# Loading one of three inputs four tokens to a partition, and a weight in smaller pieces

## The chip, the cores and the metric

The kernel runs on one core of a Trainium2 chip. The metric is the device time of one execution in microseconds (us), lower is better. The median of three runs of the kernel before is 166.17 us.

## What is computed

Two layers follow each other, an RWKV-style linear attention and an MLP-Mixer block. Batch is 4, heads 8, sequence 768, head size 48 (so the model width is 384), hidden sizes 256 (over tokens) and 1536 (over channels).

```python
for t in range(S):                       # attention, per batch and head
    kt, vt, rt = k[:, :, t], v[:, :, t], r[:, :, t]
    cur = einsum('bhd,bhe->bhde', u * kt, vt)
    y[:, :, t] = einsum('bhd,bhde->bhe', rt, state + cur)
    state = w[..., None] * state + einsum('bhd,bhe->bhde', kt, vt)
x = y.transpose(0, 2, 1, 3).reshape(B, S, H * D)
u2 = x + (relu(x.T @ w_tok1) @ w_tok2).T # mixing over tokens
out = u2 + relu(u2 @ w_ch1) @ w_ch2      # mixing over channels
```

All inputs and the output are float32. k, r and v lie in memory as [batch, head, token, 48], so one token of one head is a run of 192 bytes.

## The kernel before

The attention is cut into 24 *units*, six per batch, of 128 tokens and all 8 heads each. A unit loads k, r and v, each with one DMA (direct memory access transfer) from the SyncE queue, into a tile of 128 partitions by 384 numbers: one token per partition, its eight heads side by side. Each such load is 1024 runs of 192 bytes, 192 KB in all. The decay w is put into two tables, `wn` for k and `wp` for r, with one column block per chunk position; both are made on ScalarE at the start, as exponentials of ln w (`lnw`) times a token number (`iota`). The products k·wn and r·wp go, in bfloat16, into a tile called `kpr` (steps `kp` and `rp`, on GpSimd or VectorE). For units 0 to 13 TensorE transposes the two halves of `kpr` into `tr_ps` (steps `trk`, `trr`), and ScalarE copies the result to `rk`, for some units in two halves (`rkk`, `rkr`) and for the others in one. For units 14 to 23 a transposing DMA does it. From `rk` come the masked scores (`at_ps`, `AT`), the output `y_ps` and the state `kv_ps`, `S`; `x_b` is the unit's result. v becomes `vb` in bfloat16 on ScalarE.

When a batch's six units are through, its token mixing follows (`h_ps` with `wtok`, `h1r`, then `uT` and `u_sb`), and then the channel mixing in two halves of three chunks: 12 steps `z` per half (`z_ps`, 128 of the 1536 hidden columns each, weights `wch1`), `zr` (relu), and `h` steps with `wch2` (`h_ps`), whose sum is stored (`osb`, `out_dram`).

The order is not written by hand. `graph` lists the steps with estimated durations, waits and ranks, `Plan.run` simulates them, and the steps are emitted in that order; each engine then works strictly through its own list. The SyncE list of loads is fixed by `CFG["transfers"]`. The weights are cast from float32 to bfloat16 by DMAs that GpSimd issues, each placed behind a step named in `CFG["wafter"]`: `wtok1` and `wtok2` behind the loads of unit 4, then the pieces of `wch1` and `wch2` behind `rp5`. They use a queue of their own (q0 in the profile, the SyncE loads are q1), and all queues share the core's 16 DMA engines. The load of k of unit 6 is held back until `y5` is through (`hold`), and a load of unit n+8 waits until unit n's buffer is free.

Where all engine calls go through one helper, all instructions carry one line number in the profile (L512); they are told apart by the names of their tiles.

Of the kernel before, what the change touches and what calls it, by code (L numbers as in the profile page):

```python
# [13 lines left out]
f32 = mybir.dt.float32  # L14
bf16 = mybir.dt.bfloat16
i32 = mybir.dt.int32
# [15 lines left out]
LATER = tuple(range(2 * C, NU))  # L32

# [127 lines left out]
MM = 0.1625  # L161
# [6 lines left out]
def graph(do, cfg):  # L168

    p = Plan(4, cfg.get("busy_until", dict(ACT=3.9, DVE=3.6, POOL=5.0, PE=5.4)), cfg.get("in_flight", 8), cfg.get("relax_from", 0.0))  # L170
# [10 lines left out]
    lnw = p.add("lnw", [("ACT", 0.49, 0.6)], rank=-100, emit=do("lnw"))  # L181
# [13 lines left out]
    for n, (kind, i) in enumerate(cfg["transfers"]):  # L195
# [11 lines left out]
    wx, wi = {}, {}  # L207

    def weight(i, after):
        wi[i] = s = p.add(f"i:w{i}", [("POOL", 0.9, cfg.get("wseen", 1.0), True)], after, rank=-50, emit=do("weight", i))  # L210
        took = cfg.get("wtime", (3.0, 2.6, 3.1, 7.7, 3.1) if 5 not in cfg["wafter"] else (3.0, 2.6, 3.1, 3.9, 3.1, 3.9))[i]
        wx[i] = p.transfer(f"x:w{i}", s, took, took + 1.0, -1.0)

    for i in cfg["wafter"]:
# [3 lines left out]
    for u in range(NU):  # L218
        b, c = divmod(u, C)
        r = unit_rank(u)  # L220
        f = cold[u] if u < len(cold) else 1.0
        tab = tables[c % G]
        t_at, t_y, t_yS = cfg.get("pe_times", ((0.36, 0.25, 0.185),) * 2)[u >= C]
        old = xs.get(u - LEAD)
        d = cfg.get("dve_late", {}).get("kr", 0.5) if u >= cfg.get("early", 6) else cfg.get("kr0", 0.5)
        DK = DVE2 + (d,)
        d = cfg.get("dve_late", {}).get("yd", 0.5) if u >= cfg.get("early", 6) else cfg.get("yd0", 0.5)
# [10 lines left out]
        if u in turned:  # L238
            s = p.add(f"i:t{u}", [("SP", 1.35, 1.4)], [kp, rp], rank=-2000, emit=do("turn_unit", u))
            rk = p.transfer(f"x:t{u}", s, 1.56, 2.2, 0.0)  # L240
        else:
# [80 lines left out]
    for b in range(B):  # L322
        r, m, o = mix_rank(b) + cfg.get("mix", (0.0,) * B)[b], mlp_rank(b), out_rank(b)
        f = 1.0
        h = None
# [16 lines left out]
        uT, some = [], []  # L342
# [27 lines left out]
        for sg in range(2):  # L370
            zr = []
            for j in range(NJ):
                old = downs[2 * b + sg - 3] if 2 * b + sg >= 3 else []
                z = p.add(f"z{b}_{sg}_{j}", [("PE", 3 * MM, 3 * MM + 0.13)], old + uT[3 * sg:3 * sg + 3] + [wx[2] if j < NJ // 2 else wx[4]], take=True, rank=m + 0.1 * sg + 0.001 * j, emit=do("z", b, sg, j))
# [57 lines left out]
    + [('u', 13)]  # L432
    + [('b', 0)]
    + [("u", u) for u in range(14, 24)]
    + [('w', 0), ('w', 1), ('w', 2), ('w', 4), ('w', 3), ('w', 5)],
# [6 lines left out]
    parts=2,  # L442
    cold=(1.8, 1.8, 1.8, 1.3),
    xload={6: 0.33},
    wtime=(3.0, 2.6, 3.1, 5.2, 3.1, 3.9),
    raw=(0, 1, 5, 8, 11),
    rk_two=(0, 1, 2, 3, 4, 6),
    mix=(0.0, 0.0, -1.0, -2.6),
# [17 lines left out]
def kernel(  # L466
# [13 lines left out]
    nc = tc.nc  # L480
# [5 lines left out]
    dch = moe_w_ch1.shape[1]  # L486
    by_pe = CFG.get("by_pe", range(NU))
    direct = CFG.get("direct", ())

    const = ctx.enter_context(tc.tile_pool(name="const", bufs=1))  # L490
    wts = ctx.enter_context(tc.tile_pool(name="wts", bufs=1))
# [29 lines left out]
    def h3(t):  # L521
        return t.rearrange("p (h d) -> p h d", h=H)
# [2 lines left out]
    idle = const.tile([128, 512], bf16, name="idle")  # L525
    dve.memset(idle, 0.0)
    row = const.tile([1, dm], f32, name="row")
    rows = const.tile([2 * HP, 2, P], f32, name="rows")
# [10 lines left out]
    w_ps = psM.tile([128, dm], f32, name="w_ps", tag="m")  # L539
# [6 lines left out]
    pe.matmul(w_ps, ones, row, start=True, stop=True)  # L546
    warm(CFG.get("warm", (1, 10))[1])

    iota_i = const.tile([128, 2, G], i32, name="iota_i")
# [4 lines left out]
    ident = const.tile([128, 128], bf16, name="ident")  # L554
    make_identity(nc, ident)
    mask = const.tile([128, 128], f32, name="mask")
    pool.memset(mask, 1.0)
    pool.affine_select(
# [34 lines left out]
    lnw = const.tile([128, dm], f32, name="lnw")  # L593
    wn = const.tile([128, G, dm], f32, name="wn")
    wp = const.tile([128, G, dm], f32, name="wp")
    wu_sb = const.tile([128, 2, HP], f32, name="wu_sb")
# [9 lines left out]
    def wp_(eng, g):  # L606
        act.activation(wp[:, g, :], lnw, Exp, scale=iota[:, 0, g:g + 1])

    def wu(eng):
# [24 lines left out]
    def load(eng, nm, i):  # L634
        b, c = divmod(i, C)
        t = lpool.tile([128, dm], f32, name=f"ld_{nm}")
        ins = sp.dma_start(h3(t), SRC[nm][b, :, ts(c, T), :].rearrange("h s d -> s h d"))
        if i in CFG.get("hold", {}) and nm == "k":
            first = INS["".join(map(str, CFG["hold"][i]))]
            tc.add_manual_dep(ins.ins, first.ins.name,  # L640
                              mybir.DependencyInfo(mybir.DependencyClass.Sync, mybir.DependencyReason.DATA),
                              reason="weights first")
        loaded[nm, i] = t

    def weight(eng, i):
        t, src = [(wtok1, moe_w_tok1), (wtok2, moe_w_tok2), (wch1, moe_w_ch1), (wch2, moe_w_ch2), (wch1, moe_w_ch1), (wch2, moe_w_ch2)][i]
        cols = {2: slice(0, dch // 2), 4: slice(dch // 2, dch)}.get(i, slice(None))
# [11 lines left out]
        ENG[eng].tensor_mul(kprs[i % NB][:, 0, :, 0:D], h3(loaded["k", i]), h3(wn[:, i % G, :]))  # L659

    def rp(eng, i):
        ENG[eng].tensor_mul(kprs[i % NB][:, 1, :, 0:D], h3(loaded["r", i]), h3(wp[:, i % G, :]))

    def vb(eng, i):
        L[i]["vb"] = apool.tile([128, dm], bf16, name="vb")
        INS[f"vb{i}"] = act.copy(L[i]["vb"], loaded["v", i])

# [27 lines left out]

    def rk(eng, i):
        L[i]["rk"] = apool.tile([128, 2, HP, T], bf16, name="rk")
        (act.copy if eng == "ACT" else dve.tensor_copy)(L[i]["rk"], L[i]["tr"])

    def rkp(eng, i, j):  # L700
        if "rk" not in L[i]:
            L[i]["rk"] = apool.tile([128, 2, HP, T], bf16, name="rk")
        (act.copy if eng == "ACT" else dve.tensor_copy)(L[i]["rk"][:, j], L[i]["tr"][:, j])

    def atq(eng, i, q):
        if q == 0:
# [234 lines left out]
    def do(kind, *args):  # L941
        return lambda eng: STEPS[kind](eng, *args)
# [53 lines left out]
```

## Time and profile before

| | |
|---|---|
| median of 3 runs (lowest, highest) | 166.17 us (164.99, 168.54) |
| the profiled execution's span | 166.5 us |
| TensorE busy | 156.8 us, 94% of the span |
| VectorE, ScalarE, GpSimd busy | 106.8, 87.2, 65.3 us |
| DMA: bytes moved, packets | 26.26 MB, 97427 |

The profile lists for the profiled execution no time beside its span. Busy time is the sum of an engine's instructions; the chain of waits follows the last instruction back to what released it, step by step. "SPq" and "POOLq" are DMA instructions as their engines issue them, "DMA" is the transfer itself, and a DMA share of 1.0 means that 16 DMA engines had packets under way on average. A wait in square brackets stands behind the instruction that ended it, with what released it.

### The profile page before, as it was taken

To read this page: it belongs to the slowest core of one execution; us is meant where nothing else is said; L and a number is where in the kernel's file an instruction comes from. 1 tells how busy PE (TensorE), PEld (TensorE's weight loads), DVE (VectorE), ACT (ScalarE), POOL (GpSimd) and SP (SyncE) were. 2 spreads that over 40 slices of the span, in tenths; PEclk is the share of its full clock that TensorE was granted. 3 is DMA by queue.
4 is the path that set the end of the run, shared out by engine and by line. 5 is a ranking of instruction groups with operands and counts; after the bars stand their busy time and mean duration, and the time that the engine had idled before them with its cause. 6 is when DMAs were issued, how large, how long until landed. Compare 5 with 4: busy or idle time off the path is not lost.

```text
span 166.5 us, 3791 instructions
## 1 busy us (share of the span) xinstructions
PE 156.8 (94%) x1462; PEld 100.6 (60%) x1464; DVE 106.8 (64%) x219; ACT 87.2 (52%) x182; POOL 65.3 (39%) x80
## 2 busy tenths in 40 slices
PE   6797999599999999999999999999999999999991
PEld 1377764356677666666666665666656655665671
DVE  5189996300459989899989889977885582021031
ACT  3996743279198636579804452069154502904900
POOL 7839970000009647386785857103840000000000
PEclk9999999789999999999999999999999999999999
DMA  5999999999699899999999994999990028012012
GB/s 100 215 213 210 159 187 176 188 184 168 131 208 287 158 192 216 217 230 182 198 192 169 230 158 106 188 235 222 171 240 6 4 50 218 16 51 94 0 47 94
DMA packets 97427, 26.26 MB, mean 158 GB/s; under 512 B 90753, under 2 KB 97410, under 8 KB 97410
## 3 DMA queue, kind: packets, MB, share of 16 engines
q1 hardware_dynamic: 93920, 22.88, 67.2%
q0 software_dynamic: 3488, 3.15, 12.3%
q8 instruction: 11, 0.18, 0.5%
q14 instruction: 6, 0.05, 0.1%
q10 hardware_dynamic: 2, 0.00, 0.0%
HBM read 20.65 MB, written 4.72 MB: 152 GB/s over the span
## 4 chain that ended last, share of the span: by engine, by line
PE 79%; DMA 8%; POOL 5%; ACT 3%; issue 2%; DVE 1%; SPq 1%; POOLq 0%
PE h_ps L512 31%; PE z_ps L512 29%; DMA wch<-in_moe_w_ch_dram 6%; PE y_ps L512 4%; PE at_ps L512 4%; PE hT_ps L512 3%; PE tr_ps L512 3%; POOL kpr L512 3%; PE kv_ps L512 2%; DMA ld_v<-in_v_dram 2%; PE t_ps L512 1%; ACT rk L512 1%; POOL wtok L512 1%; SPq L512 1%; POOL yd L512 0%
## 5 line engine op out<-in xcount | busy, mean ns | idle before, releaser
L512 ACT ACTIVATE zr<-z_ps 128x384 bf16<-128x384 f32 x94 | 45.5, 492 | 47.5 <-PE z_ps L512 47.3
L512 PE MATMUL z_ps<-uT,wch 128*128 128x384 bf16 x288 | 53.6, 331 | 2.0 <-DMA wch<-in_moe_w_ch_dram 2.0
L512 PE MATMUL h_ps<-wch,zr 128*128 128x384 bf16 (+1 forms) x300 | 52.5, 319 | 0.0
L512 PEld LDWEIGHTS <-wch 128*128 128x128 bf16 x288 | 27.0, 99 | 18.8 <-DMA wch<-in_moe_w_ch_dram 2.4
L512 PEld LDWEIGHTS <-zr 128*128 128x128 bf16 x300 | 27.9, 98 | 15.5 <-issue 0.2
L512 POOL TENSOR_TENSOR yd<-vb,adg 128x384 f32<-128x384 bf16 x18 | 15.5, 860 | 46.5 <-ACT adg L512 27.9
L512 DVE TENSOR_TENSOR AT<-at_ps,mask 128x512 bf16<-128x512 f32 x43 | 27.9, 682 | 0.7 <-PE at_ps L512 0.6
L512 DVE TENSOR_TENSOR osb<-u_sb,h_ps 128x384 f32<-128x384 bf16 (+1 forms) x22 | 11.7, 533 | 23.4 <-PE h_ps L512 23.3
L512 POOL TENSOR_TENSOR kpr<-ld_r,wp 128x384 bf16<-128x384 f32 x16 | 16.6, 1036 | 5.3 <-ACT wp L512 2.8
L512 ACT COPY rk<-tr_ps 128x512 bf16<-128x512 bf16 (+1 forms) x20 | 15.0, 756 | 4.9 <-PE tr_ps L512 4.5
L512 PEld LDWEIGHTS <-kpr 128*128 128x128 bf16 x192 | 13.7, 107 | 6.0 <-POOL kpr L512 2.6
L512 DVE TENSOR_TENSOR x_b<-y_ps,yd 128x384 bf16<-128x384 f32 x24 | 13.2, 552 | 5.2 <-PE y_ps L512 5.1
L512 POOL TENSOR_TENSOR kpr<-ld_k,wn 128x384 bf16<-128x384 f32 x15 | 15.2, 1011 | 1.8 <-DMA ld_r<-in_r_dram 0.7
L512 PEld LDWEIGHTS <-rk 48*128 48x128 bf16 (+1 forms) x272 | 11.0, 99 | 6.4 <-issue 2.7
L512 ACT CAST vb<-ld_v 128x384 bf16<-128x384 f32 x24 | 12.3, 511 | 4.3 <-POOL kpr L512 3.1
L512 PE MATMUL tr_ps<-ident,kpr 128*128 128x128 bf16 x112 | 12.1, 245 | 2.4 <-ACT rk L512 1.4
L512 DVE TENSOR_TENSOR S<-kv_ps,bm 128x384 bf16<-128x384 f32 x13 | 7.2, 551 | 6.0 <-PE kv_ps L512 5.8
L512 DVE TENSOR_TENSOR u_sb<-x_b,hT_ps 128x384 bf16<-128x384 bf16 x21 | 10.4, 546 | 0.9 <-PE hT_ps L512 0.9
L512 PEld LDWEIGHTS <-wtok 128*128 128x128 bf16 x90 | 8.0, 98 | 4.8 <-issue 0.6
L512 PEld LDWEIGHTS <-AT 128*128 128x128 bf16 x192 | 8.4, 98 | 3.4 <-DVE AT L512 0.8
L512 PE MATMUL at_ps<-rk 48*128 48x128 bf16 x192 | 10.2, 229 | 0.2 <-ACT rk L512 0.2
L512 PE MATMUL h_ps<-x_b,wtok 128*128 128x384 bf16 x48 | 10.2, 326 | 0.0
(81 smaller groups left out, 145.4 us busy)
## 6 DMA issues: line engine op xcount, KB each, us to landing
ld_k<-in_k_dram SPq DMA_DIRECT2D x24, 192.0 KB, 3.8
ld_r<-in_r_dram SPq DMA_DIRECT2D x24, 192.0 KB, 3.8
ld_v<-in_v_dram SPq DMA_DIRECT2D x24, 192.0 KB, 3.8
out_dram<-osb SPq DMA_DIRECT2D x23, 192.0 KB, 2.6
wch<-in_moe_w_ch_dram POOLq DMA_DIRECT2D x4, 576.0 KB, 14.2
wtok<-in_moe_w_tok_dram POOLq DMA_DIRECT2D x2, 384.0 KB, 6.4
u_bc<-in_u_dram SPq DMA_DIRECT2D x1, 192.0 KB, 5.0
out_dram<-osb SPq DMA_DIRECT2D x2, 96.0 KB, 1.6
```

Source lines behind the costliest of these rows:

```text
L512: ins = tc.keep_in_program_order(f(*args, **kw))
```

## The change

For units 0 to 13 (`split`), r is loaded by two DMAs instead of one. Each takes four of the eight heads (every second one) and puts four consecutive tokens of one head behind each other in a partition: 128 partitions are 4 heads by 32 groups of tokens, and a run in memory is 4 x 48 numbers, 768 bytes. The source pattern of each is 4 heads, 32 groups, 192 numbers. In consequence

- the table `wp` gets the same layout (`wr`): a second small load of w (`row4`), a matmul with a matrix `quarter` that spreads four rows over the partitions, a second logarithm `lnr`, token numbers `iota_r`, three products on VectorE and an exponential in place. For units 14 to 23 the table is written again in the old layout (`wp_as_read`), from step `vb` of units 13 to 15.
- the product `rp` writes through a view of four dimensions, and the copy of r's half of `rk` puts the tokens back in order. `rk` of units 0 to 13 is always copied in two halves.

The first half of `wch1` (768 columns) is asked for as two pieces of 384 columns (weights 2 and 6); the first three `z` steps wait for the first alone.

```diff
+R = HP                                   # 4
...
-                z = ... [wx[2] if j < NJ // 2 else wx[4]] ...
+                z = ... [wx[2] if j < NJ // 4 else wx[6] if j < NJ // 2 else wx[4]] ...
...
-    wafter={0: 'x:r4', 1: 'x:r4', 2: 'rp5', 4: 'kp5', 3: 'rp5', 5: 'rp5'},
+    wafter={0: 'x:r4', 1: 'x:r4', 2: 'rp5', 6: 'rp5', 4: 'kp5', 3: 'rp5', 5: 'rp5'},
...
+    split=range(0, 14),
...
     act.dma_start(out=row, in_=w.rearrange("h d -> (h d)")[None, :])
+    act.dma_start(out=row4, in_=w.rearrange("(a q) d -> a (q d)", q=2))
...
+    pe.matmul(w_ps[:, dm:], quarter..., row4, start=False, stop=True, ...)
...
     def lnw_(eng):
-        act.activation(lnw, w_ps, Ln)
+        act.activation(lnr..., w_ps[:, dm:], Ln)
+        act.activation(lnw, w_ps[:, 0:dm], Ln)
+        for g in range(G):
+            dve.tensor_mul(wr[:, g], lnr..., iota_r[:, g]...)
...
     def wp_(eng, g):
+        act.activation(wp[:, g, :], wp[:, g, :], Exp)
...
-        ins = sp.dma_start(h3(t), SRC[nm][b, :, ts(c, T), :].rearrange("h s d -> s h d"))
+        src = SRC[nm][b, :, ts(c, T), :]
+        if nm == "r" and i in split:
+            for q in range(2):
+                ins = sp.dma_start(t[:, ts(q, dm // 2)], src.rearrange("(a q) (s j) d -> q a s (j d)", q=2, j=R)[q])
+        else:
+            ins = sp.dma_start(h3(t), src.rearrange("h s d -> s h d"))
...
     def rkp(eng, i, j):
...
+        if j == 1 and i in split:
+            to, src = to.rearrange("p a (t j) -> p a t j", j=R), src.rearrange("p j (a t) -> p a t j", a=HP)
```

The head of SyncE's list, with the loads of the first two units (a row's last number is the shape that the first operand takes), before:

```order
L512 DMA ld_k<-in_k_dram 128x8x48
L512 DMA ld_r<-in_r_dram 128x8x48
L512 DMA ld_v<-in_v_dram 128x8x48
L512 DMA ld_k<-in_k_dram 128x8x48
L512 DMA ld_r<-in_r_dram 128x8x48
```

and the same place now:

```order
L515 DMA ld_k<-in_k_dram 128x8x48
L515 DMA ld_r<-in_r_dram 128x1x192 x2
L515 DMA ld_v<-in_v_dram 128x8x48
L515 DMA ld_k<-in_k_dram 128x8x48
L515 DMA ld_r<-in_r_dram 128x1x192 x2
```

Each load of r has become two, in the same place; nothing else moves on this queue, through all 14 units.

On GpSimd, the stretch from the products of unit 4 to the weights (kpr_126 belongs to unit 4, kpr_118 to unit 5), before:

```order
L512 TENSOR_TENSOR kpr_126<-ld_k,wn 128x8x48
L512 DMA wtok_146<-in_moe_w_tok_dram 128x6x256
L512 TENSOR_TENSOR kpr_126<-ld_r,wp 128x8x48
L512 DMA wtok_147<-in_moe_w_tok_dram 128x2x768
L512 TENSOR_TENSOR kpr_118<-ld_k,wn 128x8x48
L512 TENSOR_TENSOR kpr_118<-ld_r,wp 128x8x48
L512 DMA wch_148<-in_moe_w_ch_dram 128x3x768 x2
L512 DMA wch_149<-in_moe_w_ch_dram 128x6x384 x2
```

and now (kpr_138 and kpr_130 are the same two buffers):

```order
L515 TENSOR_TENSOR kpr_138<-ld_k,wn 128x8x48
L515 DMA wtok_159<-in_moe_w_tok_dram 128x6x256
L515 TENSOR_TENSOR kpr_138<-ld_r,wp 128x2x4x48
L515 DMA wtok_160<-in_moe_w_tok_dram 128x2x768
L515 TENSOR_TENSOR kpr_130<-ld_k,wn 128x8x48
L515 TENSOR_TENSOR kpr_130<-ld_r,wp 128x2x4x48
L515 DMA wch_161<-in_moe_w_ch_dram 128x3x384 x2
L515 DMA wch_161<-in_moe_w_ch_dram 128x3x768
L515 DMA wch_162<-in_moe_w_ch_dram 128x6x384 x2
```

The order is the same; one weight transfer has become two, still behind r's product of unit 5. On TensorE the only other move is that one group of three transposes into `t_ps` now stands behind the second `z` step instead of ahead of it.

More of the change, by code (lines that the diff above doesn't have):

```diff
@@ L210, in weight @@
         wi[i] = s = p.add(f"i:w{i}", [("POOL", 0.9, cfg.get("wseen", 1.0), True)], after, rank=-50, emit=do("weight", i))
-        took = cfg.get("wtime", (3.0, 2.6, 3.1, 7.7, 3.1) if 5 not in cfg["wafter"] else (3.0, 2.6, 3.1, 3.9, 3.1, 3.9))[i]
+        took = cfg["wtime"][i]
         wx[i] = p.transfer(f"x:w{i}", s, took, took + 1.0, -1.0)
@@ L444 @@
     xload={6: 0.33},
-    wtime=(3.0, 2.6, 3.1, 5.2, 3.1, 3.9),
+    wtime=(3.0, 2.6, 1.55, 5.2, 3.1, 3.9, 1.55),
     raw=(0, 1, 5, 8, 11),
@@ L488 @@
     direct = CFG.get("direct", ())
+    split = CFG.get("split", ())
     const = ctx.enter_context(tc.tile_pool(name="const", bufs=1))
@@ L527 @@
     row = const.tile([1, dm], f32, name="row")
+    row4 = const.tile([HP, 2 * D], f32, name="row4")
     rows = const.tile([2 * HP, 2, P], f32, name="rows")
@@ L538 @@
     idle_ps = psM.tile([128, 512], f32, name="idle_ps", tag="m")
-    w_ps = psM.tile([128, dm], f32, name="w_ps", tag="m")
+    w_ps = psM.tile([128, dm + 2 * D], f32, name="w_ps", tag="m")
     def warm(n):
@@ L545 @@
     warm(CFG.get("warm", (1, 10))[0])
-    pe.matmul(w_ps, ones, row, start=True, stop=True)
+    pe.matmul(w_ps[:, 0:dm], ones, row, start=True, stop=True, skip_group_check=True)
+    ident = const.tile([128, 128], bf16, name="ident")
+    make_identity(nc, ident)
+    quarter = const.tile([HP, HP, T // R], f32, name="quarter")
+    dve.tensor_copy(quarter, ident[0:HP, 0:HP].unsqueeze(2).to_broadcast([HP, HP, T // R]))
+    pe.matmul(w_ps[:, dm:], quarter.rearrange("p a t -> p (a t)"), row4, start=False, stop=True, skip_group_check=True)
     warm(CFG.get("warm", (1, 10))[1])
@@ L553 @@
     dve.tensor_copy(iota, iota_i)
-    ident = const.tile([128, 128], bf16, name="ident")
-    make_identity(nc, ident)
+    iota_ri = const.tile([128, G, R], i32, name="iota_ri")
+    for a in range(HP):
+        pool.iota(iota_ri[a * (T // R):(a + 1) * (T // R)], pattern=[[T, G], [1, R]], base=-MID, channel_multiplier=R)
+    iota_r = const.tile([128, G, R], f32, name="iota_r")
+    dve.tensor_copy(iota_r, iota_ri)
     mask = const.tile([128, 128], f32, name="mask")
@@ L595 @@
     wp = const.tile([128, G, dm], f32, name="wp")
+    wr = wp.rearrange("p g (q j d) -> p g q j d", q=2, j=R)
+    lnr = const.tile([128, 2, D], f32, name="lnr")
+    natural = set()
     wu_sb = const.tile([128, 2, HP], f32, name="wu_sb")
@@ L600, in lnw_ @@
     def lnw_(eng):
-        act.activation(lnw, w_ps, Ln)
+        act.activation(lnr.rearrange("p q d -> p (q d)"), w_ps[:, dm:], Ln)
+        act.activation(lnw, w_ps[:, 0:dm], Ln)
+        shape = [128, 2, R, D]
+        for g in range(G):
+            dve.tensor_mul(wr[:, g], lnr.unsqueeze(2).to_broadcast(shape), iota_r[:, g].unsqueeze(1).unsqueeze(3).to_broadcast(shape))
     def wn_(eng, g):
@@ L606, in wp_, with wp_as_read @@
     def wp_(eng, g):
+        act.activation(wp[:, g, :], wp[:, g, :], Exp)
+    def wp_as_read(g):
+        natural.add(g)
         act.activation(wp[:, g, :], lnw, Exp, scale=iota[:, 0, g:g + 1])
@@ L661, in rp @@
     def rp(eng, i):
-        ENG[eng].tensor_mul(kprs[i % NB][:, 1, :, 0:D], h3(loaded["r", i]), h3(wp[:, i % G, :]))
+        assert (i % G in natural) == (i not in split)
+        if i in split:
+            ENG[eng].tensor_mul(kprs[i % NB][:, 1, :, 0:D].rearrange("p (j q) d -> p q j d", q=2),
+                                loaded["r", i].rearrange("p (q j d) -> p q j d", q=2, j=R), wr[:, i % G])
+        else:
+            ENG[eng].tensor_mul(kprs[i % NB][:, 1, :, 0:D], h3(loaded["r", i]), h3(wp[:, i % G, :]))
     def vb(eng, i):
+        if i + 1 not in split and len(natural) < G:
+            wp_as_read((i + 1) % G)
         L[i]["vb"] = apool.tile([128, dm], bf16, name="vb")
@@ L697, in rk @@
         L[i]["rk"] = apool.tile([128, 2, HP, T], bf16, name="rk")
-        (act.copy if eng == "ACT" else dve.tensor_copy)(L[i]["rk"], L[i]["tr"])
+        if i in split:
+            for j in range(2):
+                rkp(eng, i, j)
+        else:
+            (act.copy if eng == "ACT" else dve.tensor_copy)(L[i]["rk"], L[i]["tr"])
     def rkp(eng, i, j):
@@ L702, in rkp @@
             L[i]["rk"] = apool.tile([128, 2, HP, T], bf16, name="rk")
-        (act.copy if eng == "ACT" else dve.tensor_copy)(L[i]["rk"][:, j], L[i]["tr"][:, j])
+        to, src = L[i]["rk"][:, j], L[i]["tr"][:, j]
+        if j == 1 and i in split:
+            to, src = to.rearrange("p a (t j) -> p a t j", j=R), src.rearrange("p j (a t) -> p a t j", a=HP)
+        (act.copy if eng == "ACT" else dve.tensor_copy)(to, src)
     def atq(eng, i, q):
```

8 lines of the change are left out of this document (4 added, 4 removed).

## The prediction

> **What bounds the kernel now.** The chain of waits comes first, the work that ended last, in order of time (start, duration, what):
>
> ```profile
> 0.82 0.46 SPq L512
> 1.34 0.56 SPq L512
> 1.95 3.63 DMA ld_v<-in_v_dram
> ...
> 19.91 0.94 POOL kpr L512
> 20.86 10.02 DMA wch<-in_moe_w_ch_dram
> 30.92 0.85 PE z_ps L512 x3
> ...
> 145.57 5.85 PE h_ps L512 x36
> 151.42 5.85 PE z_ps L512 x36
> 157.27 5.89 PE h_ps L512 x48
> ```
>
> Two parts are to be seen. Until 30.92 the chain runs over loads and products and ends in the 10 us of the first `wch` transfer. From there TensorE carries it nearly alone, so what happens later counts only where TensorE has to stop. Next the table by stages: for each stretch the engines' busy time, then the granted TensorE clock, the DMA share and GB/s.
>
> ```profile
> 10.00:20.00 10.00, 9.00 (x125) 7.54 (x125) 9.60 (x21) 8.40 (x21) 7.77 (x9) 1.00 1.04 188
> ...
> 40.00:50.00 10.00, 10.00 (x94) 6.68 (x93) 3.84 (x7) 6.01 (x14) 0.41 (x1) 1.00 0.82 159
> 50.00:60.00 10.00, 10.00 (x148) 7.18 (x147) 9.45 (x22) 6.10 (x13) 7.84 (x9) 1.00 0.94 213
> 60.00:70.00 10.00, 9.74 (x136) 6.66 (x133) 8.65 (x17) 5.97 (x11) 5.71 (x6) 1.00 1.00 212
> ```
>
> The DMA engines are full from 10 to 20 us (share 1.04) and nearly full from 40 to 70, while the units that the change touches are loaded. From 10 to 20 us a load of 192 KB (0.1966 MB) costs all 16 engines 0.1966/0.188/1.04 = **1.0 us**. That number can be tested. The first v landed at 1.95 + 3.63 = 5.58; r of unit 5 is 14 loads later, so it should land at 19.6, and its product stands in the timeline (start, duration, engine, instruction, idle time before it) at 19.91:
>
> ```profile
> 19.91 0.99 POOL L512 TENSOR_TENSOR kpr<-ld_r,wp 128x384 bf16<-128x384 f32 x1
> ...
> 22.93 0.51 ACT L512 CAST vb<-ld_v 128x384 bf16<-128x384 f32 x1 [0.42 <-DMA ld_v<-in_v_dram]
> ```
>
> The first six units therefore run at the pace of the DMA engines, 3.0 us each. So the question is what the new form of r's load costs these engines.
>
> **What a load of r costs now.** Three rows of the queues: packets, MB, share of the 16 engines' span.
>
> ```profile
> q1 hardware_dynamic: 93920, 22.88, 67.2%
> q0 software_dynamic: 3488, 3.15, 12.3%
> ...
> q10 hardware_dynamic: 2, 0.00, 0.0%
> ```
>
> For long rows the only price is that of the weights on q0: 3.15 MB of bfloat16 written, twice that read, in 12.3% of 166.5 = 20.5 us, that is 307 GB/s. At that pace 192 KB cost 16 engines 0.64 us, against 1.0 in rows of 192 bytes. That is the gain that the longer rows offer, 0.36 us per load, if the load is spread over 16 engines.
>
> I think that it is not. q10 is ScalarE's queue, and its only transfer before is `row`, a source of one row of 384 numbers: two packets in all. So a transfer with one outer row kept to one engine (one packet of data, one that reports the end), though it could have been cut, while those with 128 outer rows fill the 16. The new source pattern is 4 heads, 32 groups, 192 numbers: its outermost count is 4, where it was 128. I read the rows so that the outermost count decides and r's two DMAs use **four engines**, the same four each time. The bytes then cost these four 4 x 0.64 = **2.56 us** per r load. The bounds: 1.0 us, if four engines moved as much as 16 do in short rows, and 4.0, if long rows were no faster per byte than short ones. 2.56 lies nearest to a row and is taken.
>
> By the Trainium skill, page "DMA: Bandwidth & Descriptors", section "Why a DMA increments its semaphore by 16 and not by 1", a transfer runs on the largest number of engines up to 16 that divides the slowest dimension, not counting ones, of both patterns; for 4 and 128 that would be 4 engines. The two packets of q10 agree with it; no run here shows a pattern with 4 yet.
>
> A unit of k, r and v then costs the four engines 1.0 + 2.56 + 1.0 = 4.56 us instead of 3.0, and the other twelve 2.0. A load has landed when its last engine is through, and each engine works through its rows in order, so the four set the pace: 1.56 us more for each of 14 units.
>
> **Stage one, units 0 to 5.** v of unit 0 lands at 5.58 + 1.56 = 7.14, v of unit 4 four units later, at 25.4, k of unit 5 at 26.4 and r of unit 5 at 28.9. Something now comes ahead of it. GpSimd asks for the two `wtok` transfers behind the products of k and of r of unit 4:
>
> ```profile
> 16.29 0.90 POOL L512 DMA_DIRECT2D wtok<-in_moe_w_tok_dram  x1
> 17.20 1.01 POOL L512 TENSOR_TENSOR kpr<-ld_r,wp 128x384 bf16<-128x384 f32 x1
> 18.15 0.78 POOL L512 DMA_DIRECT2D wtok<-in_moe_w_tok_dram  x1
> ```
>
> Before, they were asked for at 16.29 and 18.15, and hit mostly v of unit 5, which came at 22.93 instead of 20.6. Now k and r of unit 4 land at 21.8 and 24.4, so the two are asked for at about 22.8 and 25.4, both ahead of r of unit 5. Each reads 0.79 MB, 2.56 us at 307 GB/s. Between nothing (28.9) and both wholly (34.0) I take the first wholly and half of the second: r of unit 5 lands at 32.7 and its product ends at 33.7, where it ended at 20.9. From that product to the point where TensorE is ready for the first `z` it took 8.0 us, up to the end of the last row here:
>
> ```profile
> 27.76 1.14 PE L512 MATMUL hT_ps<-h1r,wtok 128*128 128x384 bf16 x6
> 30.92 0.85 PE L512 MATMUL z_ps<-uT,wch 128*128 128x384 bf16 x3 [2.02 <-DMA wch<-in_moe_w_ch_dram]
> ```
>
> So TensorE is ready at 41.7. The first `wch` piece is 0.59 MB; asked for at 33.7, it needs 1.9 us beside few loads and is there before 41.7. The smaller piece thus takes away the 2.02 us wait, but the wait is gone anyhow, since the unit itself is late. The first `z` starts at 41.7 instead of 30.92: **+10.8 us** (7.0 to 12.1 by the bounds of the weights' place).
>
> **Stage two, units 6 to 13.** Eight more loads of r cost the four engines 8 x 1.56 = 12.5 us. What can hide them is the time for which a load lay ready. Issues of r for units 8 and 13, their products, and the median time to landing:
>
> ```profile
> 44.46 0.84 SPq L512 DMA_DIRECT2D ld_r<-in_r_dram  x1
> 60.97 0.73 SPq L512 DMA_DIRECT2D ld_r<-in_r_dram  x1
> ...
> 50.67 1.08 POOL L512 TENSOR_TENSOR kpr<-ld_r,wp 128x384 bf16<-128x384 f32 x1 [0.25 <-PE at_ps L512]
> 67.67 1.00 POOL L512 TENSOR_TENSOR kpr<-ld_r,wp 128x384 bf16<-128x384 f32 x1 [0.55 <-PE kv_ps L512]
> ...
> ld_r<-in_r_dram SPq DMA_DIRECT2D x24, 192.0 KB, 3.8
> ```
>
> They landed at about 48.3 and 64.8 and were used 2.4 and 2.9 us later. Besides, the engines were free for 1.8 and 0.6 us between 40 and 60 (shares 0.82 and 0.94). So 12.5 - 2.9 - 2.4 = **7.2 us** remain, and TensorE, whose order is fixed, stops for them at the transposes of these units with its `z` and `h` work behind. Bounds: 6 x 1.56 - 5.3 = 4.1 us, if units 6 and 7, whose loads run beside weights, lose nothing, and 12.5, if nothing is hidden.
>
> **The clock.** After the 2.02 us stop the granted clock fell:
>
> ```profile
> 30.00:32.00 2.00, 1.08 (x8) 0.79 (x9) 0.00 (x0) 0.19 (x1) 0.00 (x0) 0.81 1.21 188
> 32.00:34.00 2.00, 2.00 (x12) 1.21 (x11) 0.72 (x2) 0.95 (x3) 0.00 (x0) 0.50 1.26 185
> 34.00:36.00 2.00, 2.00 (x12) 1.12 (x11) 0.00 (x0) 1.51 (x4) 0.00 (x0) 0.83 1.28 184
> ```
>
> 0.2 of the 1.08 us, 1.0 of the next 2.00 and 0.34 of the last are lost, 1.5 us. The late `z` start will pay this as now; for stage two I add one more such dip, **+1.5** (0 to three dips, 4.5).
>
> **Edits costed at nothing.** The start gains a small load, a matmul, a logarithm and three VectorE products. Nearest rows:
>
> ```profile
> 3.91 0.49 ACT L512 ACTIVATE lnw<-w_ps 128x384 f32<-128x384 f32 x1 [1.28 <-PE w_ps L512]
> ...
> 7.29 0.56 DVE L512 TENSOR_TENSOR S<-kv_ps,bm 128x384 bf16<-128x384 f32 x1 [4.19 <-PE kv_ps L512]
> ```
>
> The logarithm, with a quarter of the columns, is at most 0.49, the products 3 x 0.56 = 1.7 us in VectorE's 4.19 us of idleness. Before the 1.56 us by which r of unit 0 is late they do not show; were r on time, they would cost up to 1 us. The copies in two halves, with r's half in strides, lie between nothing and twice a half copy on ScalarE, the products `rp` in four dimensions between 1.00 and the 1.25 us that the slowest of them took; units now 4.56 us apart hide both. Three more exponentials of about 0.6 us around units 13 to 15 run beside a TensorE that has `z` work: nothing, at most 1.8. SyncE's 14 more issues of about 0.4 us fit between loads that take the engines 1.0 us.
>
> **Sum.** 166.5 (the span; it is 0.3 from the median of the runs, 166.17, so no correction is made) + 10.8 + 7.2 + 1.5 = **186.0 us**. With the bounds, 166.5 + 7.0 + 4.1 + 0 = 177.6 and 166.5 + 12.1 + 12.5 + 4.5 = 195.6: its own range is 178 to 196.
>
> **Rivals.** *All 16 engines* (faster). If the hardware spreads the 128 destination rows instead of the 4 source rows, six loads of r save 6 x 0.36 = 2.2 us ahead of the first `wch` piece, which itself is 1.9 us shorter; 4.1 us cover the 2.02 us stop at 30.92 wholly. Next in line is the end of `hT_ps` at 28.9, so 2.0 us go, and the clock dip of 1.5 with them: 163.0. Later loads change nothing, as TensorE is busy. For it speaks that the two packets of q10 are one transfer with one row, a thin basis; it decides from about ten engines on, where r's 0.64 x 16 us of work, shared by ten, cost each no more than the 1.0 us of before. The Trainium skill speaks for this side with the same page's section "Specifications", where 512 bytes is the least size for full rate; the 188 against 307 GB/s agree in direction. *Stage two hidden* (slower, less): should loads of units 8 to 13 be asked for early enough after the late `z`, only stage one stays, 166.5 + 10.8 = 177.3. *The dear end* (slower, more): at 4.0 us per load, a unit takes 6.0, r of unit 5 lands at 37.6 + 3.8 for the weights, the first `z` starts at 50.4 (+19.5), and stage two becomes 8 x 3.0 - 2.9 - 2.4 = 18.7: 206 with the clock.
>
> **Chances.** Forecast 0.60, stage two hidden 0.15, dear end 0.04, 16 engines 0.21. The last lies at the edge of 2%, which is what a measurement of this kernel can tell from no change (3.3 us), so I split it: faster 0.11, within 2% 0.10, and slower 0.79. The range reaches down to 163 and up to 196; below it lies half of the fast rival (0.10), above it the dear end and little more.
>
> **What would show it.** Right: loads of r taking some 4 to 6 us to land at the start, GpSimd and ScalarE waiting for `ld_r` and `ld_v` in units 1 to 5 at a pace of about 4.6 us, a lower GB/s from 10 to 30 us than the 188 now, the first `z` near 42 and waiting for no `wch`, and TensorE waits at `tr_ps` between 55 and 90. Wrong: a first `z` near 29, GB/s above 200 in the first 20 us, or a first `z` at 42 with no further stops. The step most in doubt is the one from two packets of one transfer to four engines.

## The result, and the profile after

The changed kernel takes **181.94 us** (median of four runs, 181.13 to 182.12) against 165.88 for the kernel before (four runs, 164.99 to 168.54): a ratio of **1.0987**, 95% interval 1.0947 to 1.1027. The profiled execution has a span of 180.2 us, against 166.5 before. In the later comparisons, with 25, 20 and 7 runs of the kernel before, its median is 165.2 to 165.4. Four executions clearly longer than the others of their kernel (168.54 and 529.77 us of the kernel before, 169.37 and 181.58 of two others) are in the medians of this document and not in the ratios.

The queues first (packets, MB, share of the 16 engines' span), since the prediction hung on how many engines a load of r uses:

```profile
q1 hardware_dynamic: 83056, 22.88, 58.2%
q0 software_dynamic: 3888, 3.15, 12.1%
...
q10 hardware_dynamic: 10, 0.00, 0.0%
```

The same bytes move on q1, 10,864 packets fewer than the 93,920 before. The 14 loads that went had 14 x 1024 packets of data and 14 x 16 that report the end, one from each of 16 engines; the new ones bring 14 x 256 packets of 768 bytes and their own reports. 93,920 - 14,336 - 224 + 3,584 = 82,944, so 112 reports are left for 28 transfers: **four each**, so four engines each. q10 grew from 2 to 10 by `row4`, a source of four rows: four packets of data and four reports, the same count once more. The times of the single packets in the trace agree: while r's packets of 768 bytes are under way, no more than four are so at once for 84% of the time, and more than six almost never. Whether it is the same four engines for every load, the trace doesn't tell.

The chain of waits, with its shares by engine and line ahead of the pieces (start, duration, what):

```profile
by line: PE h_ps L515 24.5%; SPq L515 23.5%; PE z_ps L515 20.1%; DMA ld_r<-in_r_dram 11.5%; PE y_ps L515 2.9%; PE at_ps L515 2.9%; PE hT_ps L515 2.4%; POOL kpr L515 2.3%; issue 1.7%; PE kv_ps L515 1.3%; ACT rk L515 1.1%; PE tr_ps L515 0.7%;
...
4.45 2.91 SPq L515
9.33 2.31 SPq L515
...
13.86 2.13 SPq L515
17.96 2.35 SPq L515
...
22.47 2.01 SPq L515
24.53 6.23 DMA ld_r<-in_r_dram
30.98 1.00 POOL kpr L515
```

Where the chain before ended its first part in a weight, it now runs over SyncE's issues up to the load of r of unit 5. The long pieces are the issues of r's first half, at 4.45, 9.33, 13.86, 17.96 and 22.47: one unit every 4.5 us, SyncE held up in each. r of unit 5 lands at 30.76. The table by stages (as in the prediction: PE, PEld, DVE, ACT and POOL busy, then the clock, the DMA share and GB/s):

```profile
10.00:20.00 10.00, 7.15 (x86) 5.79 (x85) 7.70 (x17) 6.49 (x16) 3.29 (x4) 1.00 0.67 150
...
40.00:50.00 10.00, 9.88 (x69) 6.04 (x67) 3.13 (x7) 8.24 (x18) 0.00 (x0) 1.00 1.15 182
50.00:60.00 10.00, 10.00 (x110) 6.86 (x108) 5.02 (x10) 5.70 (x14) 0.83 (x1) 1.00 0.67 146
60.00:70.00 10.00, 8.77 (x113) 6.05 (x111) 8.71 (x18) 5.68 (x12) 5.70 (x6) 1.00 0.72 178
70.00:80.00 10.00, 6.88 (x93) 4.51 (x92) 6.26 (x13) 4.40 (x10) 6.08 (x7) 1.00 0.60 131
```

From 10 to 20 us the DMA share fell from 1.04 to 0.67 and the rate from 188 to 150 GB/s: the engines as a whole do less while more waits for them. From 70 to 80 TensorE loses 3.1 of 10 us. Two waits name the culprit (us in total, times, longest), and the timeline of TensorE shows where they fall: the first `z`, then the transposes of the second stage (its idle time and releaser in brackets).

```profile
POOL kpr L515 <- DMA ld_r<-in_r_dram: 20.3, 11, 3.2
...
ACT vb L515 <- DMA ld_v<-in_v_dram: 13.4, 10, 2.4
```

```profile
41.00 0.65 PE L515 MATMUL z_ps<-uT,wch 128*128 128x384 bf16 x3
...
65.48 0.40 PE L515 MATMUL tr_ps<-ident,kpr 128*128 128x128 bf16 x4 [1.13 <-POOL kpr L515]
71.26 0.40 PE L515 MATMUL tr_ps<-ident,kpr 128*128 128x128 bf16 x4 [0.80 <-POOL kpr L515]
75.60 0.40 PE L515 MATMUL tr_ps<-ident,kpr 128*128 128x128 bf16 x4 [1.38 <-POOL kpr L515]
79.87 0.40 PE L515 MATMUL tr_ps<-ident,kpr 128*128 128x128 bf16 x4 [0.95 <-POOL kpr L515]
84.03 0.40 PE L515 MATMUL tr_ps<-ident,kpr 128*128 128x128 bf16 x4 [0.52 <-POOL kpr L515]
```

Before, the same two waits, GpSimd's for r and ScalarE's for v, were 0.7 and 0.8 us. The first `z` starts at 41.00 instead of 30.92 and waits for no `wch`; the five stops of the second stage sum to 4.8 us.

### The profile page after: what moved, and what is told of

It reads as the page before. It is cut to its first block, busy times and chain, and to the rows that moved or that the text cites. A ratio compares the mean times of both kernels' runs of the same rounds, so it can differ in the third digit from the quotient of the medians.

```text
span 180.2 us, 3850 instructions
## 1 busy us (share of the span) xinstructions
PE 160.1 (89%) x1464; PEld 103.0 (57%) x1466; DVE 110.9 (62%) x224; ACT 89.2 (50%) x194; POOL 67.3 (37%) x85
## 3 DMA queue, kind: packets, MB, share of 16 engines
q1 hardware_dynamic: 83056, 22.88, 58.2%
## 4 chain that ended last, share of the span: by engine, by line
PE 55%; SPq 23%; DMA 11%; POOL 3%; ACT 3%; issue 2%; DVE 1%; POOLq 0%; ACTq 0%
PE h_ps L515 25%; SPq L515 23%; PE z_ps L515 20%; DMA ld_r<-in_r_dram 11%; PE y_ps L515 3%; PE at_ps L515 3%; PE hT_ps L515 2%; POOL kpr L515 2%; PE kv_ps L515 1%; ACT rk L515 1%; PE tr_ps L515 1%; POOL yd L515 1%; ACT wp L515 1%; ACT vb L515 0%; PE t_ps L515 0%
## 5 line engine op out<-in xcount | busy, mean ns | idle before, releaser
L515 PE MATMUL z_ps<-uT,wch 128*128 128x384 bf16 x288 | 52.5, 326 | 0.2
L515 POOL TENSOR_TENSOR yd<-vb,adg 128x384 f32<-128x384 bf16 x18 | 15.7, 874 | 37.7 <-ACT adg L515 22.8
L515 PE MATMUL tr_ps<-ident,kpr 128*128 128x128 bf16 x112 | 13.1, 254 | 13.9 <-POOL kpr L515 9.8
L515 ACT COPY rk<-tr_ps 128x512 bf16<-128x512 bf16 x28 | 15.5, 587 | 11.5 <-PE tr_ps L515 11.1
L515 PEld LDWEIGHTS <-rk 48*128 48x128 bf16 (+1 forms) x272 | 11.8, 104 | 6.6 <-issue 3.3
L515 PE MATMUL h_ps<-x_b,wtok 128*128 128x384 bf16 x48 | 11.4, 356 | 0.0
L515 PE MATMUL at_ps<-rk 48*128 48x128 bf16 x192 | 10.8, 240 | 0.4 <-ACT rk L515 0.3
L515 DVE TENSOR_TENSOR kpr<-ld_k,wn 128x384 bf16<-128x384 f32 x9 | 6.2, 693 | 7.0 <-DMA ld_k<-in_k_dram 6.8
```

The costliest lines, as they stand in the source:

```text
L515: ins = tc.keep_in_program_order(f(*args, **kw))
```

## Experiments

Every kernel below is compared with runs of the kernel before on the same chip. The questions: is it the four engines, the other edits, or the weight pieces; and would the loads have gained anything on 16 engines.

**The pattern turned.** The only thing that has to change for 16 engines is the order of the source's dimensions, 32 groups ahead of 4 heads; the tables and the copies follow it (partition = 4 x group + head).

```diff
-src.rearrange("(a q) (s j) d -> q a s (j d)", q=2, j=R)[q]
+src.rearrange("(a q) (s j) d -> q s a (j d)", q=2, j=R)[q]
-to, src = ..., src.rearrange("p j (a t) -> p a t j", a=HP)
+to, src = ..., src.rearrange("p j (t a) -> p a t j", a=HP)
 # quarter: [a, t] -> [t, a]; iota_r by a matmul of a 0/1 matrix with token numbers
```

> The changed kernel with the source pattern of r turned round: 32 groups outermost, then 4 heads (partition = 4 x group + head instead of 32 x head + group). Still two DMAs per r load, 768-byte runs, the copies in strides, the new table. Theory (the outermost count of the source sets the number of engines; four caused the loss): 32 lets 16 engines work, 28 loads then report from 16 engines each instead of 4, so q1 has 28 x 12 = 336 packets more than the 83056 of the changed kernel; a unit's loads cost 1.0 + 0.64 + 1.0 = 2.6 us on every engine, the first z starts at about 29, no transpose waits for ld_r between 60 and 85 us, span about 163 us. Rival (the two DMAs per load on SyncE, the strided copies or the longer start caused the loss): they are all still there, so the span stays at 176 to 182 us.

166.14 us, ratio 1.0041 (1.0010 to 1.0072). The queue:

```profile
q1 hardware_dynamic: 83392, 22.88, 64.7%
```

336 packets more than the change, which is 28 x 12: the same rows, with 16 reports for each transfer instead of four. One transposed pair of letters, with the tables and copies that follow from it, moves 15.8 us. So the order of the source's dimensions it was, and with it the four engines. But its first `z` starts at 30.41, and with its loads on all engines the kernel is still no faster than before. The next runs ask why.

**The same with the weight in one piece.**

> As e1, but the first half of the first up weight asked for in one piece of 768 columns, as in the kernel before. Theory: six loads of r save 6 x 0.36 = 2.2 us of DMA time ahead of the weight, just the 2.02 us for which TensorE stopped, so the pieces add little: 0 to 1 us slower than e1. Rival (the weight is still the last to come, because the loads of v and k keep the engines full): the first z waits up to 1.9 us more, and a clock dip of up to 1.5 us follows: 2 to 3.4 us slower than e1.

166.36 us, ratio 1.0056 (1.0020 to 1.0093). As expected of the theory, the pieces add next to nothing there, 0.2 us.

**The weight pieces alone**, on the kernel before, twice (the second time beside the later runs):

```diff
-    + [..., ('w', 2), ('w', 4), ('w', 3), ('w', 5)]
+    + [..., ('w', 2), ('w', 6), ('w', 4), ('w', 3), ('w', 5)]
-        cols = {2: slice(0, dch // 2), ...}
+        cols = {2: slice(0, dch // 4), 6: slice(dch // 4, dch // 2), ...}
```

> The kernel before with the two weight pieces alone, r loaded as before. Theory: the first piece reads 0.59 MB less than the half, 1.9 us at 307 GB/s, so the wait of 2.02 us ahead of the first z falls to about 0.1 and the dip of the granted clock behind it (1.5 us) goes or shrinks: 162.5 to 164.5 us of span. Rival (the second piece is then late, z steps 4 to 6 wait for it, or the interleaving with k of unit 6 holds the first piece back): 165 to 166.5.

> The kernel before with the two weight pieces alone, once more with more rounds beside the others: 164.4 to 165.3 us, the first z near 29.6 with no wait for the weight, and a ratio to the kernel before of 0.993 to 0.998. Rival, the earlier 0.4% was chance: a ratio of 1.000.

164.87 us, ratio 0.9957 (0.9929 to 0.9985), and 164.48, ratio **0.9949** (0.9923 to 0.9974). A small gain, and a real one: both intervals lie below 1. The timeline of TensorE in the first of the two runs, and its stage from 30 to 40 us:

```profile
29.64 0.65 PE L512 MATMUL z_ps<-uT,wch 128*128 128x384 bf16 x3
...
31.52 6.99 PE L512 MATMUL z_ps<-uT,wch 128*128 128x384 bf16 x42
```

```profile
30.00:40.00 10.00, 9.88 (x71) 6.14 (x70) 1.99 (x5) 8.25 (x17) 0.00 (x0) 1.00 1.26 196
```

The 2.02 us wait for `wch` is gone, the first `z` starts 1.3 us earlier, and the clock stays at 1.00, where before it was 0.81, 0.50 and 0.83 in the six us from 30. The end comes 2.9 us earlier in this execution (163.6), but only 0.8 us in the medians of the second comparison: the profiled execution of the kernel before was one of its long ones. Its span, 166.5, is above its median time of 165.3, and of its first four executions only the one of 168.54 us is longer than that span, while in every other kernel's profiled execution here the span is 1.7 to 2.0 us below the time. Nor is its dip of the clock the rule: 1.5 us lost of 166 lower the mean granted clock to 0.991, and it was 0.990 in that execution, but 0.996 to 1.000 in all 52 later ones of the kernel before. So the dip, and perhaps the wait, belong to that one execution, and what the pieces take away in a usual one, no trace here shows. In the second run the first `z` came at 28.36, so two executions of one kernel differ by 1.3 us there, and smaller differences of first `z` between single traces below say little. The pieces alone are the only version here whose interval against the kernel before lies below 1.

**The change for units 0 to 5 alone.** Units 6 to 13 load r as before; the old table is written in the first `z` step.

```diff
-    split=range(0, 14),
+    split=range(0, 6),
```

> The changed kernel with r in the new form for units 0 to 5 alone; the table is written back to the old layout beside the first z steps. Theory: stage one is late by the same 10 us (first z at 41), stage two runs as before, without the 5 us of stops at transposes between 60 and 85 us: span 174 to 176 us. Rival (the loads of units 6 to 13 catch up in both, and what is lost after the first z comes from the copies in two halves or the weights): within 1 us of the changed kernel's 180.2.

175.19 us, ratio 1.0570 (1.0509 to 1.0630): 6.7 us less than the change. Its timeline keeps one long stop, at the same place as in the change (units 0 to 5), and has none at the transposes after the first `z`:

```profile
30.91 0.40 PE L515 MATMUL tr_ps<-ident,kpr 128*128 128x128 bf16 x4 [3.73 <-POOL kpr L515]
39.62 0.65 PE L515 MATMUL z_ps<-uT,wch 128*128 128x384 bf16 x3
```

Its first `z` came 1.4 us before that of the change, in the part that is alike in both; two more kernels below with the same loads had it at 40.1. So 1 us of the 6.7 may be scatter of the first stage, and the second stage costs 5 to 7 us.

**The slow loads alone.** The kernel before, with the two weight pieces and the change's source pattern, nothing else.

```diff
+if nm == "r" and i < 14:
+    for q in range(2):
+        sp.dma_start(t[:, ts(q, dm // 2)], src.rearrange("(a q) (s j) d -> q a s (j d)", q=2, j=4)[q])
```

> The same with the source pattern of the change, 4 heads outermost (four engines), and nothing else of the change but the two weight pieces; left out as before: tables and order of tokens. Theory: behind the slow loads the changed kernel's start, products and copies cost nothing, so this gives the time of the changed kernel: 181.2 to 182.6 us, the first z near 41.0. Rival, they cost 1 to 2 us there too: 179.5 to 181.

181.42 us (181.15 to 181.84), ratio 1.0979 (1.0956 to 1.1002), 83,056 packets on q1. The whole loss of the change is in these two DMAs per unit: the tables, the exponentials, the products in four dimensions and the copies in strides cost nothing behind them.

**The change with the weight in one piece.**

> The changed kernel with the first up weight asked for in one piece of 768 columns. Theory: the first six units are so late that nothing waits for the weight: 181.4 to 182.5 us, the first z near 41 with no wait for wch. Rival, the smaller piece saves part of a wait in the changed kernel too: 183 to 184 us and a wait at the first z.

181.09 us (181.01 to 181.88), first `z` at 40.06, with no wait. The time is a little below the expected range. The smaller piece does nothing for the changed kernel, as it is late anyway.

**Fast loads alone, two issues a unit.** As the run of the slow loads, with the pattern `q s a (j d)`.

> The weight in two pieces, and r of 14 units loaded with 32 groups outermost (sixteen engines); everything behind the loads is as in the kernel before. Left out: the tables and the order of tokens that fit this form, so r's products are those of other tokens. Theory: in the kernel before, the first six units do not wait for their loads (0.7 us of waiting in GpSimd, 0.8 in ScalarE), so a load that costs 0.64 instead of 1.0 us brings little: the first z 29.0 to 29.6 and 164.0 to 164.9 us, against 164.9 with the pieces alone. Rival, the prediction's own reading, that the first six units run at the pace of the DMA engines: 6 x 0.36 = 2.2 us earlier, the first z at 27.5 to 28.4 and 162.7 to 163.6 us.

167.79 us (166.85 to 168.46), ratio 1.0133 (1.0098 to 1.0169): slower than before, which neither side expected. Still, it differs from the run of the slow loads alone in the order of two letters and nothing else, and that pair of runs gives the price of the four engines at the same number of issues: 181.42 against 167.79, 13.6 us. Its chain of waits, with the shares of the first 60 us:

```profile
by line: SPq L512 27.2%; PE z_ps L512 19.8%; PE h_ps L512 18.1%; DMA ld_r<-in_r_dram 8.5%; PE at_ps L512 5.1%; PE tr_ps L512 4.3%; PE y_ps L512 3.6%; issue 2.3%; PE fill_ps L512 2.3%; PE kv_ps L512 2.1%; POOL kpr L512 1.7%; PE hT_ps L512 1.
...
15.06 0.59 SPq L512
15.70 1.74 SPq L512
17.48 0.59 SPq L512
18.12 5.07 DMA ld_r<-in_r_dram
23.35 1.00 POOL kpr L512
```

SyncE's queue is the chain up to there. In the first six units it issues one DMA after the other, none shorter than 0.58 us after the first, and four a unit instead of three. The second half of r of unit 5 is issued at 18.12, behind the first `wtok` transfer, which GpSimd asked for at 17.01, and lands 5 us later; with three issues a unit (the weight pieces alone) r of unit 5 was asked for at 14.55, ahead of both `wtok`.

The turned version has the same four issues a unit and doesn't lose this. Its tables make GpSimd ask for `wtok` later, and both halves of r of unit 5 are asked for ahead of it:

```profile
15.33 1.24 SPq L515 DMA_DIRECT2D ld_r<-in_r_dram  x2
...
17.80 0.89 POOL L515 DMA_DIRECT2D wtok<-in_moe_w_tok_dram  x1
```

Its chain of waits begins with the small matmuls and products of the tables, and SyncE is not in the first part of it.

**Fast loads alone, one issue a unit.** The 16-engine pattern allows one DMA for all eight heads.

```diff
+    sp.dma_start(t.rearrange("p (q x) -> p q x", q=2), src.rearrange("(a q) (s j) d -> s a q (j d)", q=2, j=4))
```

> The loads of r in the sixteen-engine form, as in the run that had nothing but these loads and the two weight pieces, but each unit of r asked for by one instruction (32 groups, 4 heads, 2 halves, 192 numbers) instead of two. Left out as there: the tables and the order of tokens that fit. Theory: it was SyncE's issues, four a unit at 0.59 to 0.94 us, back to back up to 18.07 us, that made that run slower than the kernel before; with three a unit the first z starts at 28.6 to 29.7 and the time is 163.8 to 165.0 us. Rival, the longer rows are no faster where the other loads run beside them (the wait for r of unit 5 stays): first z near 33 and 167 to 168 us.

165.22 us (164.53 to 166.47), ratio 0.9988 (0.9959 to 1.0016): 1.45% or 2.4 us less than with two issues, and nothing more; it is a little above the expected 163.8 to 165.0, and no better than the weight pieces without the fast loads (164.48 beside it). GpSimd's timeline shows why:

```profile
8.13 0.99 POOL L512 TENSOR_TENSOR kpr<-ld_r,wp 128x384 bf16<-128x384 f32 x1
12.28 1.00 POOL L512 TENSOR_TENSOR kpr<-ld_r,wp 128x384 bf16<-128x384 f32 x1 [3.16 <-ACT wp L512]
...
17.65 1.01 POOL L512 TENSOR_TENSOR kpr<-ld_r,wp 128x384 bf16<-128x384 f32 x1
18.60 0.78 POOL L512 DMA_DIRECT2D wtok<-in_moe_w_tok_dram  x1
19.40 1.01 POOL L512 TENSOR_TENSOR kpr<-ld_k,wn 128x384 bf16<-128x384 f32 x1
20.36 1.00 POOL L512 TENSOR_TENSOR kpr<-ld_r,wp 128x384 bf16<-128x384 f32 x1
```

GpSimd waits 3.16 us for a table that ScalarE makes late (2.8 us in the kernel before), and from 12.28 works almost without a gap to the product of unit 5 at 20.36; in the kernel before it ended at 20.90, here at 21.36. No wait for r is left in it, and none to gain from. The chain of waits leaves the loads after v of unit 0 and runs over ScalarE's tables and copies, TensorE's transposes and VectorE's scores.

**The tables alone.** The start of the turned version (its extra small load, matmuls, logarithm and three VectorE products), with r loaded and used as before; the products' result is overwritten.

> r is loaded and used as in the kernel before, the weight is asked for in two pieces, and the start makes the extra tables of the sixteen-engine version (the small load, two small matmuls, the logarithm of 192... columns and three VectorE products), whose result is overwritten. Theory: it is this start, not the loads, that took back the gain of the sixteen-engine version: the first z near 30.3 (29.64 with the pieces alone, 30.41 in the sixteen-engine version), 165.7 to 166.3 us. Rival, the products in four dimensions and the copies in strides took it back: the first z near 29.7 and 164.9 us.

166.4 us (166.27 to 166.72), ratio 1.0071 (1.0055 to 1.0087), first `z` at 30.77. That is 1.5 to 1.9 us above the weight pieces alone, and about what the turned version loses to them (1.3 to 1.7). VectorE in it:

```profile
4.74 0.17 DVE L515 COPY iota_r<-w_ps 128x12 f32<-128x12 f32 x1 [2.69 <-PE w_ps L515]
...
6.16 3.02 DVE L515 TENSOR_TENSOR wp<-lnr,iota_r 128x384 f32<-128x384 f32 x3
```

A copy waits 2.69 us for the new small matmuls, with the clearing of `kpr` queued behind it. The three products then take 0.48, 1.34 and 1.35 us, the last two with GpSimd at work beside them. So the turned version's start accounts for its loss against the pieces alone.

**One issue, and a start with the tables spread out.** The turned version whole, with one DMA per unit, a second PSUM tile so that `lnw` need not wait for the new matmuls, and each product made when its exponential is due.

> The sixteen-engine version whole, with one issue per unit of r, and a start in which the logarithm of the first table no longer waits for the new small matmuls and each VectorE product of the tables is made when its exponential is due. Theory: the start is what the sixteen-engine version lost, 1.2 us, and about half of it comes back: the first z near 29.8 to 30.2 and 165.0 to 165.7 us. Rival, the loads gain once the issue is gone: below 164.5 us. A second rival, the start costs the same wherever its products lie: 166.0 to 166.5.

167.34 us (167.06 to 167.43), ratio 1.0111 (1.0076 to 1.0146): worse than any expectation. Spread out, the products came onto ScalarE's path:

```profile
6.72 0.52 ACT L515 ACTIVATE wp<-wp 128x384 f32<-128x384 f32 x1 [1.45 <-DVE wp L515]
```

ScalarE waits 1.45 us for the first of them, which took 1.38 us beside a product of GpSimd's, with all its later work behind it; GpSimd's product of r of unit 0 starts at 7.32 (6.14 before), and all six units follow, up to a first `z` at 31.30. At this start the order in which small steps stand on one engine is worth more than r's loads.

## Why the prediction was right

Forecast 186.0 us, measured 181.94; 79% stood on slower, with four engines as the reason.

- **Four engines, 4.56 us a unit.** Right. GpSimd's products of r start 4.3 us apart in units 0 to 4 (7.72 to 25.02) and 4.56 us apart in units 8 to 13 (60.15 to 82.97), and the packet counts give 4 and 16 reports per transfer. The step in doubt, from the two packets of one small transfer to the count of engines, held. How the 4.56 divide is less sure: r's packets were under way for 3.2 us per load, from the first to the last of the four engines, where 2.56 was taken. No run shows the split into 1.0, 2.56 and 1.0, and that the sum came out to the second digit in stage two is in part luck. The Trainium skill's rule on the slowest dimension (page "DMA: Bandwidth & Descriptors", section "Why a DMA increments its semaphore by 16 and not by 1") gives 4 for the change and 16 for the turned pattern, and both counts agree with it.
- **Stage one, +10.8 us.** Measured +10.1 (41.00 against 30.92) by these two traces. The two `wtok` were asked for at 22.77 and 25.96, as forecast (22.8 and 25.4), but r of unit 5 landed at 30.8 instead of 32.7. Its product started 6.0 us after unit 4's (30.98 and 25.02), so beyond a unit's pace of 4.3 to 4.6 the weights in its way cost about 1.5 us, not the 3.84 of one and a half of them. TensorE then needed 9.0 us from the product's end to its first `z` instead of 8.0. The clock dip now lies in this stretch, and the stretch goes with it: 8.8 to 9.0 us in the five traces that have a dip there, 7.5 to 8.4 in the seven others that have none. No `wch` wait at the end: right.
- **Stage two, +7.2 us.** Between the first `h` (49.71 against 40.95) and the `hT_ps` step behind unit 13's transposes (84.26 against 69.93) the change falls another 5.6 us behind, 0.6 of which it makes up by the end: 4.9. The comparison of medians with units 0 to 5 alone gives 6.7. The place, the transposes, was right. The price per unit was too high: the sum took 1.56 us, from units 3.0 us apart, but GpSimd's products of r of units 8 to 13 stood 3.4 us apart before (50.67 to 67.67), so at 4.56 each costs 1.16, and the five steps 5.8. The reserve of 5.3 us that was taken off adds those of two units, though the second may hold the first.
- **The clock, +1.5 us.** Wrong in sign by the trace. I added a dip for the second stage; its stops of 0.52 to 1.38 us brought none. And the dip of the late `z` start is gone with the wait for `wch`; another stands ahead of it (below), inside stage one's 10.1. The dip behind the first `z` was priced from the one long execution and is in no other of the kernel before (mean clock 0.996 and more). From the first `z` to the first `h` the change takes 8.7 us, the kernel before 10.0: -1.3, not +1.5.
- **The sum.** 166.5 + 10.1 - 1.3 + 4.9 = 180.2, the span. The terms together were 5.8 us too large (0.7, 2.8 for the clock, 2.3 for stage two), and the sum left out the 1.8 us by which the time exceeds the span (181.96 and 180.2 in this execution); 186.0 - 5.8 + 1.8 = 182.0. The base hid this: the span of a long execution happened to agree with the median of the times. By the medians the change costs 16.6 us, by the two traces 13.7; where the other 2.9 us lie is open, as no trace of a usual execution of the kernel before was kept. That 186.0 came within 4.1 us is in part luck: by the traces the terms were too large and the base was too small.
- **The edits at nothing.** Right under slow loads (181.42 with none of them). On time, the start of the turned version, which has one small matmul more, costs 1.5 to 1.9 us, more than the "up to 1 us" that the prediction allowed; no run shows the change's own start with loads on time.
- **"The first six units run at the pace of the DMA engines."** This reading of the kernel before was wrong, and the forecast did not suffer because 4.56 us is above any other pace. A DMA share of 1.04 and a unit every 3.0 us looked like one thing (by the issues of r it was 2.8, 1.34 to 15.12). The product at 19.91 that seemed to confirm the landing at 19.6 waits for no load: GpSimd's product of k stands straight ahead of it, at 18.95 for 1.01 us. GpSimd's and ScalarE's waits for loads were only 0.7 and 0.8 us, and loads that cost less moved nothing (165.22). The units run at the pace of small steps on ScalarE, TensorE, VectorE and GpSimd, with DMA just as busy beside them.
- **The rival of 16 engines, 163.0 us.** Its price was wrong for that reason: what the turned form gives is 166.1, no change. SyncE's 14 more issues were costed at nothing, at about 0.4 us; they take 0.58 us and more. Without the tables they cost 2.4 us (ratios of 1.0133 and 0.9988), because r of unit 5 then fell behind a `wtok`. In the turned version they cost nothing that shows: with four issues a unit it takes 166.14 us, and the tables alone with three take 166.4.

## What to carry to other kernels

Look at the outermost count of a DMA's source before its run length: rows four times as long on a quarter of the engines made each unit's loads take half as long again, and the packets of the queue tell the number of engines (data rows plus one report for each). A busy share near 1 does not make an engine the bound; before pricing a faster load, look whether anybody waits for loads, and whether the issuing queue has room for more of them. One more issue on a queue cost time here where it pushed a load that is waited for behind another transfer, and none that shows where it didn't. The gain here lay in the smallest edit, the first half of a weight asked for in two pieces: 0.5% in the medians. The wait of 2 us and the clock dip that it removed stood in a single long execution.

## What the runs showed of the hardware

**Stops of TensorE of 1.80 to 3.77 us were followed by a lower clock, but length alone doesn't decide.** Two rows of the changed kernel, behind its stop of 2.17 us before 32.03, and one of the run with fast loads and two issues, behind a stop of 2.58 us before 24.39 (PE busy first, the granted clock third from the end):

```profile
34.00:36.00 2.00, 2.00 (x14) 1.00 (x11) 1.67 (x4) 0.59 (x1) 1.94 (x3) 0.50 1.06 156
36.00:38.00 2.00, 2.00 (x27) 1.52 (x25) 0.66 (x2) 0.00 (x0) 0.00 (x0) 0.76 1.25 191
```

```profile
26.00:28.00 2.00, 2.00 (x21) 1.24 (x20) 1.78 (x4) 0.84 (x2) 2.00 (x3) 0.50 0.84 118
```

Both look like the dip before (0.81, 0.50, 0.83 behind 2.02 us), and so do those behind 3.77 and 3.73 us (the change with the weight in one piece, and six units alone). Behind the longest stop of the second stage, 1.38 us, the clock held. So it did in the changed kernel's first stage behind a stop of 1.84 us before 22.18; but in the run of the slow loads alone it fell behind one of 1.80 us, before 31.15:

```profile
76.00:78.00 2.00, 2.00 (x29) 1.26 (x28) 0.86 (x3) 1.18 (x3) 1.28 (x2) 1.00 0.98 224
...
20.00:25.00 5.00, 2.93 (x37) 2.59 (x36) 2.43 (x6) 2.79 (x6) 2.81 (x3) 1.00 0.70 139
```

```profile
32.00:34.00 2.00, 1.91 (x21) 1.11 (x20) 1.37 (x3) 1.70 (x3) 2.00 (x3) 0.67 0.78 55
34.00:36.00 2.00, 2.00 (x15) 1.17 (x13) 1.00 (x3) 0.00 (x0) 1.06 (x2) 0.50 1.28 197
```

Nor does the same program always dip: of the changed kernel's four executions, three had a mean clock of 0.991 (181.91 to 182.12 us) and one of 1.000 (181.13). What else decides, no run here tells.

**A product of VectorE and one of GpSimd at the same time are slower.** Of VectorE's products for the tables, the two beside GpSimd's products took 1.34 and 1.35 us in the run of the tables alone, and GpSimd's up to 1.32; those that ran alone or nearly so took 0.48 to 0.56 (there, and in the changed kernel), GpSimd's 1.00. It isn't always both that pay: in the run with the tables spread out VectorE's took 1.38 us and GpSimd's beside it 0.99, and where GpSimd's first product in the changed kernel overlapped VectorE's last for 0.4 us, VectorE's took 0.56 and GpSimd's 1.21.
